# First batch, first stage: a transpose by VectorE out of PSUM in place of a trip through DRAM, with loads in one queue and weights rounded in pairs

## The chip, the cores and the metric

The kernel runs on one core of one Trainium2 chip. The metric is the time on the device in microseconds (us); lower is better. The executions of one kernel agree within about 0.2% on one chip.

## The reference, cut to what matters

```python
X = np.fft.rfft(x, axis=1)                 # x: (8, 3008, 256) float32
Y = X * (filt_r + 1j * filt_i)[None]       # one filter per frequency and channel
y = np.fft.irfft(Y, n=3008, axis=1)
h = y.reshape(24064, 256) @ w_in           # w_in  (256, 2048), float64
out = (h / (1 + np.exp(-h))) @ w_out       # w_out (2048, 256), float64
```

The transform of 3008 = 47 x 64 points is done as matmuls with tables. Stage 1 transforms over the rows, `forward` and the filters work on six groups g = 0 to 5 of residues, `inverse`, `even` and `rows` go back, and stage 3 makes y. The two matmuls of the experts follow. They make up most of the program, and batches 1 to 7 of the transform are woven into them. Only batch 0 must be through its transform before the first expert matmul (px) can start. The weights come as 64-bit floats and are made 32-bit on the chip ("rounded") while batch 0 runs: 16 pieces, of which 0 to 8 are done before px.

## The kernel before: the parts that matter

Stage 1 of batch 0 wrote its result to DRAM (d1) and read it back, which is how the data changed from "row on partitions" to "n on partitions":

```python
def stage1(u):                             # u = 0..7, batch 0
    ... two matmuls into PSUM, ps[0], ps[1]
    for h in range(2):
        evac(t1[:, h], ps[h])              # VectorE or ScalarE
    for par in range(2):
        nc.gpsimd.dma_start(out=d1[par]..., in_=t1[64 * par:64 * par + 2 * NS]...)
def load_t2(g):
    for par in range(2):
        nc.sync.dma_start(out=t2s[g][64 * par:64 * par + 64], in_=d1[par, 4 * g:4 * g + 4]...)
```

The order of the start:

```python
part["load_first"]()                       # x
idle(6)                                    # dummy matmuls, for TensorE's clock: 0.75 with, 0.70 without (e7_idle)
nc.sync.dma_start(out=d_t[:, 0:8], ...)
load_filters((nc.sync, nc.sync), 0, 4)     # the filters of g = 0, 1: 16 loads
weights(0, 1, 2)                           # loads of raw weights
for u in range(8):
    part["stage1"](u)
...
for j in range(3):
    rounded(j)                             # beside the trip through DRAM
idle(16)
for g in range(NG):
    forward, multiply, add of g
    if g == 0:
        load_filters((nc.sync, nc.gpsimd), 4, 2 * NG)   # 16 loads, half of them by GpSimd
        ...; load_t2(2), load_t2(3); weights(3, 4, 5)
    ...
    if g > 0:
        inverse_rows(part, g - 1)          # inverse, even, rows of the group before
    idle(2)
    if 1 <= g <= 4:
        rounded(g + 2)
```

`rows` stores the result of a group:

```python
queue = nc.gpsimd if b > 0 or (g == NG - 1 and i == 0) else nc.scalar
queue.dma_start(out=d2[a0:a0 + 4]..., in_=qt[:, a])
```

## Time and profile before

| | before |
|---|---|
| time, median of 3 | 2646.08 us (2644.95 to 2646.61) |
| span of the profiled run | 2644.6 us |
| PE (TensorE matmul) busy | 2587.3 us, 98% |
| DVE (VectorE) / ACT (ScalarE) / POOL (GpSimd) busy | 64% / 42% / 17% |
| first multiply by a filter (VectorE, g = 0) | 44.48 us |
| first expert matmul px | 127.53 us |
| from px to the end | 2517.1 us |

TensorE is full from px on, so a gain must come from what lies ahead of px. The last sixteen matmuls of stage 1, after a wait of 3.10 us for x, start 0.63 to 0.86 us apart from 17.03 to 20.95, and 0.43 apart from there on (granted clock 0.55 from 17.0 to 20.3 and 0.96 from 20.3 to 26.0); the prediction calls the slower ones cold. The profile's views of that stretch are shown in the prediction. In a timeline line the columns are start, duration, engine, line of the kernel, operation, output<-inputs and count; a bracket says how long the engine was idle before it and what ended that.

### The profile page before, as it was taken

What the parts mean: (1) busy time and instruction counts of PE and PEld (TensorE: products, weight loads), DVE (VectorE), ACT (ScalarE), POOL (GpSimd) and SP (SyncE); (2) the same over time, 40 slices, a digit from 0 to 9 for tenths busy, and PEclk for the clock granted to TensorE, in tenths of its full rate; (3) what the DMA queues carried; (4) which work ended last, traced back from release to release, by engine and by line L of the source; (5) the groups of instructions that cost most, each with busy time, mean ns of one, the idle gap of its engine ahead of it and who ended that gap; (6) DMA issues with size and microseconds to landing.
All of it is one profiled execution on the core that took longest, in us unless ns stands there. A gap on an engine that the chain in (4) does not pass through costs nothing.

```text
span 2644.6 us, 48073 instructions
## 1 busy us (share of the span) xinstructions
PE 2587.3 (98%) x18748; PEld 2189.9 (83%) x18748; DVE 1696.9 (64%) x3576; ACT 1110.4 (42%) x3026; POOL 450.4 (17%) x694
## 2 busy tenths in 40 slices
PE   6699999999999999999999999999999999999998
PEld 3378888888888888888888888888888888888987
DVE  3676766667666666666666676666766666555554
ACT  2354444443444444444444444444444444444443
POOL 4311111311121112112111211131112111100100
PEclk8699999999999999999999999999999999999999
DMA  8542222222223123321232222222223311211000
GB/s 247 166 114 51 77 66 51 75 72 66 56 72 84 45 64 79 70 65 47 76 71 56 65 75 67 51 71 70 72 56 72 81 48 28 55 22 21 9 16 16
DMA packets 203595, 176.29 MB, mean 67 GB/s; under 512 B 122148, under 2 KB 176772, under 8 KB 202772
## 3 DMA queue, kind: packets, MB, share of 16 engines
q1 hardware_dynamic: 183080, 121.57, 19.4%
q0 software_dynamic: 17616, 48.52, 5.8%
q8 instruction: 147, 2.41, 0.4%
q10 hardware_dynamic: 2672, 3.13, 0.4%
q14 instruction: 80, 0.66, 0.1%
HBM read 98.15 MB, written 84.41 MB: 69 GB/s over the span
## 4 chain that ended last, share of the span: by engine, by line
PE 94%; DVE 2%; DMA 2%; ACT 1%; issue 1%; POOL 1%; SPq 0%; DVEq 0%; ACTq 0%; POOLq 0%
PE acc L665 43%; PE px L606 25%; PE pyz L606 19%; PE pd L495 3%; PE pc L451 2%; PE pb L418 2%; PE pf L385 1%; DMA d_t<-d_tbl 1%; PE pa L327 0%; DMA raw<-in_moe_w_out_dram 0%; PE pa L318 0%; DVE g L577 0%; DMA d<-q 0%; ACT e L761 0%; DVE w_t L577 0%
## 5 line engine op out<-in xcount | busy, mean ns | idle before, releaser
L665 PE MATMUL acc<-g,w_t 128*128 128x256 f32 (+1 forms) x5376 | 1512.6, 375 | 0.4 <-DVE g L577 0.4
L665 PEld LDWEIGHTS acc<-g,w_t 128*128 128x128 f32 x5376 | 1022.5, 190 | 114.5 <-DVE g L577 0.8
L577 DVE TENSOR_TENSOR g<-pyz,abc 128x256 f32<-128x256 f32 (+1 forms) x1152 | 479.5, 416 | 545.0 <-ACT abc L627 302.2
L577 DVE TENSOR_TENSOR g<-g 128x256 f32<-128x256 f32 (+3 forms) x1152 | 616.3, 535 | 196.6 <-ACT g L610 183.5
L606 PE MATMUL px<-ty,w_t 128*128 128x256 f32 (+1 forms) x2304 | 687.0, 380 | 0.5 <-ACT abc L627 0.5
L610 ACT ACTIVATE g<-g 128x256 f32<-128x256 f32 (+1 forms) x1152 | 472.9, 411 | 247.6 <-DVE g L577 247.6
L577 POOL TENSOR_TENSOR s<-s 128x256 f32<-128x256 f32 (+1 forms) x329 | 259.7, 807 | 1452.6 <-DVE s L683 1417.0
L606 PEld LDWEIGHTS px<-ty,w_t 128*128 128x128 f32 x2304 | 424.5, 190 | 82.4 <-issue 25.2
L606 PE MATMUL pyz<-y,w_t 128*128 128x256 f32 (+1 forms) x1536 | 453.9, 377 | 2.6 <-DVE g L577 2.6
L606 PEld LDWEIGHTS pyz<-y,w_t 128*128 128x128 f32 x1536 | 283.7, 189 | 48.2 <-DVE g L577 8.1
L621 ACT COPY abc<-px 128x256 f32<-128x256 f32 (+1 forms) x384 | 141.3, 368 | 364.9 <-PE px L606 364.9
L610 ACT ACTIVATE g<-px 128x256 f32<-128x256 f32 (+1 forms) x384 | 145.8, 380 | 307.5 <-PE px L606 307.5
L627 ACT COPY abc<-px 128x256 f32<-128x256 f32 (+1 forms) x384 | 143.8, 374 | 309.9 <-PE px L606 309.9
L606 PE MATMUL px<-y,w_t 128*128 128x256 f32 (+1 forms) x768 | 229.9, 381 | 1.0 <-ACT y L246 1.0
L606 PE MATMUL pyz<-ty,w_t 128*128 128x256 f32 (+1 forms) x768 | 225.8, 376 | 0.0
L606 PEld LDWEIGHTS px<-y,w_t 128*128 128x128 f32 x768 | 142.2, 190 | 39.9 <-ACT g L610 15.5
L606 PEld LDWEIGHTS pyz<-ty,w_t 128*128 128x128 f32 x768 | 146.1, 190 | 16.8 <-DVE g L577 0.5
L614 ACT COPY abc<-px 128x256 f32<-128x256 f32 (+1 forms) x384 | 134.9, 351 | 2.7 <-PE px L606 1.3
L244 DVE COPY y<-pd 128x376 f32<-128x376 f32 x64 | 51.6, 806 | 103.8 <-PE pd L495 103.6
L246 ACT COPY y<-pd 128x376 f32<-128x376 f32 x64 | 51.7, 809 | 94.7 <-PE pd L495 94.7
L495 PEld LDWEIGHTS pd<-wi_t,t 48*64 48x64 f32 x4096 | 68.5, 139 | 26.2 <-issue 24.2
L495 PE MATMUL pd<-wi_t,t 48*64 48x47 f32 x4096 | 76.6, 237 | 5.9 <-issue 3.5
(76 smaller groups left out, 1362.5 us busy)
## 6 DMA issues: line engine op xcount, KB each, us to landing
t<-d SPq DMA_DIRECT2D x96, 256.0 KB
t<-d SPq DMA_DIRECT2D x128, 192.0 KB
d<-q POOLq DMA_DIRECT2D x85, 256.0 KB, 2.6
out_dram<-o SPq DMA_DIRECT2D x636, 32.0 KB
d<-tf POOLq DMA_DIRECT2D x144, 96.0 KB, 2.4
d<-t POOLq DMA_DIRECT2D x52, 192.0 KB, 3.4
xr<-in_x_dram SPq DMA_DIRECT2D x6, 1472.0 KB
x_all<-in_x_dram SPq DMA_DIRECT2D x72, 96.0 KB
```

Source lines behind the costliest of these rows:

```text
L244: nc.vector.tensor_copy(out=dst, in_=src)
L246: nc.scalar.copy(out=dst, in_=src)
L418: nc.tensor.matmul(out=ps[k][32 * j:32 * j + 32, ri, :], lhsT=d_t[rows, 4 * g + at, ri, :], rhs=t2[rows, at, :], start=True, stop=True)
L451: nc.tensor.matmul(out=ps[j][64 * k:64 * k + 64, a, :], lhsT=e_t[rows, g + a, k, ri, :], rhs=zs[k][rows, ri, :], start=(a == 0 and ri == 0 ...
L495: nc.tensor.matmul(out=ps[h][c0:c0 + 64, cb, i, :], lhsT=t4s[g][rows, i, 128 * cb + c0:128 * cb + c0 + 64], rhs=wi_t[rows, :], start=True, ...
L577: eng.tensor_tensor(out=out, in0=in0, in1=in1, op=op)
L606: nc.tensor.matmul(out=out, lhsT=w_t[:, c, 0, jp], rhs=rhs, start=start, stop=True, skip_group_check=True)
L610: nc.scalar.activation(out=g[:, k, 0:n], in_=g[:, k, 0:n] if src is None else src, func=AFT.Silu)
L614: nc.scalar.copy(out=sums[:, 0, 0:n], in_=xo)
L621: nc.scalar.copy(out=sums[:, 1, 0:n], in_=xo)
L627: nc.scalar.copy(out=sums[:, 2, 0:n], in_=xo)
L665: nc.tensor.matmul(out=acc[pair][i][:, h, 0:n], lhsT=w_t[:, c, 1, jp], rhs=g[:, k, 0:n], start=(jp == 0 and h == 0), stop=last, skip_group ...
```

## The change

The intent is to take the trip through DRAM out of batch 0's stage 1. A matmul now handles 16 channels for all 32 values of n, and VectorE transposes the 32x32 squares of the result straight from PSUM to SBUF. The result of stage 1 stays in the part of the weights' buffer w_t that is filled later, and so the layout of w_t changes. All early loads but two tables (ScalarE's) now stand in one queue (SyncE's) in order of need, the weights are rounded in pairs to overlap ScalarE's steps with VectorE's, VectorE places all rounded weights (GpSimd placed 0 to 6 before), and the dummy matmuls go. The core of the diff, cut:

```diff
-    w_t = cpool.tile([128, 7, 2, NJP, 128], FP32)
+    w_t = cpool.tile([128, NJP, 7, 2, 128], FP32)
...
+        def stage1_first(k):
+            ps = bank(b, f"pa_{b}_{k}")...rearrange("p (n c) -> p n c", c=16)
+            c0 = 16 * (k % 8)
+            for i in (0,) if k < 8 else (1, 2):
+                n0, n = ((0, 32), (0, 16), (16, 16))[i]
+                nc.tensor.matmul(out=ps[:, n0:n0 + n], lhsT=wx_t, rhs=xs[i][0:96, :, c0:c0 + 16], ...)
+            nc.vector.transpose(out=us["t2"][:, :, 16 * k:16 * k + 16].rearrange("p s c -> p c s"),
+                                in_=ps.rearrange("p n c -> p c n"))
...
-    def round_weights(j):
+    def round_weights(*js):          # the steps of two weights interleaved
...
-        eng = gp if j < 7 else v
-            eng.tensor_tensor(out=dst, ...)
+            v.tensor_tensor(out=dst, ...)
...
-    idle(6)
     load_filters((nc.sync, nc.sync), 0, 4)
-    weights(0, 1, 2)
-    for u in range(8):
-        part["stage1"](u)
-    for g in range(2):
-        part["load_t2"](g)
     nc.sync.dma_start(out=e_t, in_=e_dram.ap())
-    for j in range(3):
-        rounded(j)
-    idle(16)
+    nc.sync.dma_start(out=d_t[:, 8:NS], in_=d_dram[:, 8:NS])
+    load_filters((nc.sync, nc.sync), 4, 2 * NG)
+    weights(0, 1)
+    nc.sync.dma_start(out=wi_t, in_=wi_dram.ap())
+    weights(*range(2, 9))
+    for k in range(16):
+        part["stage1_first"](k)
     for g in range(NG):
...
-        idle(2)
-        if 1 <= g <= 4:
-            rounded(g + 2)
+        if g > 2:
+            rounded(2 * g - 6, 2 * g - 5)
...
-    rounded(7)
+    rounded(6, 7)
     rounded(8)
```

## The prediction

> **What bounds the kernel now.** I read the page first, then windows of 20 us over the start, then the chain of waits and the timeline there.
>
> The page's slices and its chain of work that ended last:
>
> ```profile
> PE   6699999999999999999999999999999999999998
> DVE  3676766667666666666666676666766666555554
> ...
> PE 94%; DVE 2%; DMA 2%; ACT 1%; issue 1%; POOL 1%; SPq 0%; DVEq 0%; ACTq 0%; POOLq 0%
> ```
>
> From the third slice (132 us on, a slice is 66 us) TensorE is full; that part of the program, some 2,510 us, is the expert matmuls with the later batches woven in. The diff touches there only the layout of w_t (each stationary is still one run of 128), and four stores in place of two of batch 1's stage 1. What can move is the start, where nothing is full:
>
> ```profile
> 0.00:20.00 20.00, 15.68 (x32) 8.37 (x33) 3.79 (x7) 3.83 (x6) 6.46 (x16) 0.93 0.91 248
> 20.00:40.00 20.00, 15.09 (x77) 9.21 (x75) 7.04 (x11) 7.82 (x12) 5.71 (x10) 0.93 0.91 274
> 40.00:60.00 20.00, 8.14 (x80) 4.20 (x74) 10.06 (x17) 3.44 (x6) 16.25 (x24) 0.67 0.75 206
> 60.00:80.00 20.00, 13.43 (x136) 5.75 (x134) 8.71 (x16) 6.31 (x12) 7.15 (x10) 0.59 0.98 282
> 80.00:100.00 20.00, 12.93 (x138) 5.57 (x136) 14.41 (x27) 6.77 (x13) 12.06 (x18) 0.69 0.15 54
> 100.00:120.00 20.00, 15.58 (x231) 11.67 (x234) 14.60 (x31) 7.56 (x12) 2.96 (x5) 0.74 0.62 142
> 140.00:160.00 20.00, 19.38 (x78) 14.16 (x77) 15.63 (x36) 11.51 (x29) 2.05 (x4) 1.00 0.35 106
> ```
>
> Columns: window, length, busy time of PE, PEld, DVE, ACT, POOL, granted PE clock, DMA share, GB/s. The DMA engines carry the first 80 us, VectorE the next 40; PE's busy time there includes the dummy "idle" matmuls. The chain in order of time names what the start waited for:
>
> ```profile
> 3.03 15.56 DMA d_t<-d_tbl
> ...
> 25.65 6.21 DMA raw<-in_moe_w_out_dram
> ...
> 60.65 4.99 DMA raw<-in_moe_w_out_dram
> 65.77 0.44 DVE m L757
> ...
> 121.56 3.45 issue
> ...
> 127.53 1.19 PE px L606 x2
> ```
>
> The first expert matmul (px) starts at 127.5 us. I take this as the end of the start: each us off it comes off the run. The timeline gives the largest hole of VectorE, from the end of its work on g = 0 and 1 at 53.4 to 65.8:
>
> ```profile
> 56.34 3.62 SPq L407 DMA_DIRECT2D t<-d  x4
> 65.77 0.43 DVE L757 TENSOR_SCALAR m<-raw 128x512 uint32<-128x512 uint32 x1 [12.41 <-DMA raw<-in_moe_w_out_dram]
> ```
>
> The loads of t2 for g = 2, 3 and, behind them in the same queue, the next raw weights are issued only at 56 to 63 us, after the filters, so VectorE stands still for 12.4 us.
>
> [...]
>
> ```profile
> L244 DVE COPY y<-pd 128x376 f32<-128x376 f32 x64 | 51.6, 806 | 103.8 <-PE pd L495 103.6
> L695 DVE STREAM_TRANSPOSE o<-s 128x256 f32<-128x256 f32 x192 | 73.7, 422 | 1.4 <-issue 1.0 <-DMA out_dram<-o 0.4
> ```
>
> Contiguous copies from PSUM take 425 ns for 256 elements and 691 for 512: 1.04 ns an element and 160 fixed, so 550 for 376. The y copy, whose writes step 128 bytes, takes 806: 1.72 ns an element. A transpose of 256 elements with whole lines takes 422, as a copy. [...]
>
> **The change part by part.**
>
> *Stage 1.* Removed: 16 evictions, 16 stores of t1 (3.1 MB), 12 loads of t2 (3.1 MB). Before, t2 arrives at 36.9 to 38.2, and VectorE, busy with weights 0 to 2, starts g = 0 at 44.5. Added: 16 transposes PSUM to SBUF, 512 elements each, reading at a step of 64 bytes and writing at 1 KB. By the y copy: 160 + 512 x 1.72 = 1.04 us; I take 1.1, as the strided PSUM read is new. Before, 1.5 MB of x had landed at 10.2 us and 3.1 MB at 17.0. Now half the channels (1.5 MB in 512-byte runs) must be in first: about 11 us. The first two matmuls are cold (2 x 0.85 each), the rest 0.86, below the transpose. First transpose at 13, sixteen end at 13 + 17.6 = 30.6; forward 0 takes 1.1 to 2; VectorE starts g = 0 at about 32, 12.5 earlier.
>
> *Loads.* All that g = 0 to 5 need is now ahead in one queue. The trace issues one in about 0.62 us, and waits once eight are in flight (the sixth filter went out when the third x landed, the seventh when the fourth did). So: filters of g 0, 1 issued by 25, e_t and d_t by 26.5, the other 16 filters by 36.5, raw 0 and 1 by 39.5, and landed some 2 later. g = 2 needs its filters at about 39.6: they just make it, so the 12.4 us hole closes.
>
> *VectorE from 32 us.* A group costs 4 multiplies at 0.60 and 4 row sums at 0.41, 4.1 in all (80.34 to 84.30 in the timeline). g = 0, 1 with the wait for POOL's adds and the inverse: 7.6, so 39.6; then 43.7 and 47.8 for g = 2, 3.
>
> *Roundings.* Before, one took 3.9 to 4.8 us of VectorE's order in the g loop, most of it waiting for ScalarE's four steps, and POOL placed the result. Now for a pair: ScalarE has six steps, 0.5 + 0.74 + 0.53 + 0.75 + 0.75 + 0.74 + 0.53 = 4.5 until the second mantissa; then 0.6 + 0.4 + 0.65 + 0.65 = 2.3 of VectorE; then four placings of 0.38, moved from POOL: 1.5. Sum 8.4, and up to 1 more [...] (0.95 against 0.42 in the old rounding 4). So pairing gains about 1.3 a pair and the moved placings give it back. But weights 0 to 2, rounded before under the DRAM trip, now lie in the path: some 13 us. Walk: pair (0,1) 56.3; g = 4 60.4; (2,3) 69.9; g = 5 with two adds 75.3; (4,5) 84.3; last row sums 86.0; (6,7) with its combine 97; (8) 101.5.
>
> *Tail.* From 86 the last d2 store waits on POOL for the combine to 87.2; before, 7.1 us went from that store's issue to the first stage-3 matmul, so 94.3, inside the roundings. The y copies wait for VectorE at 101.5 and px starts about 3.5 later, at 105. The 3.45 us "issue" gap may or may not come back.
>
> Sum: 12.5 (earlier start) + 12.4 (hole) + about 3.8 (two waits of 1.9 for POOL) + about 6 (slack by the y copies) + 2 (shorter waits), less 13 for the roundings put into the path and about 1 for the placings net of pairing: 22.5 us. 2646.1 - 22.5 = 2623.6.
>
> **Rivals.** (a) *The transposes are slower than a strided copy*: PSUM read and SBUF write penalties could add. At 1.7 us each stage 1 ends near 40, and 10 of the 22 are lost: about 2634. The even fit of the y copy on one strided side speaks for the lower cost; nothing in this trace strides a PSUM read. (b) *Loads bound instead*: without the DRAM trip VectorE may meet filters or raw weights that have not landed; one issue at 0.62 for 64 KB is only about 105 GB/s. Then g = 2 or pair (0,1) waits and the gain is 12 to 18: 2630. (c) *Roundings overlap better*: nothing of DVE's order changes, but if the contention with POOL goes, each pair is near 7.5 and stage 1 ends by 27: px near 92, 2610. (d) *Hidden anyway*: were the start off the path, 2646; the chain runs through it without slack, against this. (e) *Colder TensorE* without the dummies: pb and pc cost up to 1 us more per group, mostly beside VectorE.
>
> **Range and chances.** The terms' errors (stage 1 +-5, roundings +-5, loads -6, tail +-4) give 2612 to 2637 around 2624. 2% is 53 us; the start would have to shrink to 74 us, less than my VectorE sum alone, so faster has 0.03. A loss of 53 us would need a fault in the steady part: 0.02.
>
> **What would show it.** Right: transposes of about 1.0 to 1.2 us, no t store or t2 load before px, first multiply near 32, no VectorE hole over 5 us between it and px, a rounding pair of 8 to 9.5, px near 105, the time from px to the end unchanged within 5 us. Wrong: transposes near 1.7 or 0.7; VectorE waiting for filt or raw; a slower steady part, from the layout of w_t or batch 1's stores.

## The result, and the profile after

| | before | after |
|---|---|---|
| time, median of 4 | 2645.61 us (2644.95 to 2646.61) | 2632.71 us (2631.44 to 2633.54) |
| ratio | | 0.9950, 95% interval 0.9933 to 0.9968 |
| span of the profiled run | 2644.6 us | 2631.8 us |
| PE busy | 2587.3 us | 2554.9 us |
| first multiply by a filter | 44.48 us | 31.25 us |
| first expert matmul px | 127.53 us | 113.71 us |
| px to the end | 2517.1 us | 2518.1 us |

A ratio here and below is the mean time of one kernel's fast runs over that of the kernel before in the same rounds, so it is not quite the ratio of the medians quoted. The kernel is 12.9 us faster by the medians, half a per cent. The whole gain is ahead of px (13.8 us earlier), and the steady part is the same within 1 us. The predicted 2624 was too fast by 8.7 us; the range held.

The page after, its slices of 66 us and the engines of the chain that ended last:

```profile
PE   5599999999999999999999999999999999999998
DVE  5776766667666666666666666666766666555554
...
PE 94%; DVE 2%; DMA 1%; SPq 1%; ACT 1%; issue 1%; POOL 0%; DVEq 0%; ACTq 0%; POOLq 0%
```

TensorE has less to do in the first two slices (the dummies are gone), and the rest is as before. "SPq", the queue of SyncE, now has 1% of the chain where it rounded to 0% before, a first hint of what went otherwise than predicted. The same windows of the start (window, length, busy time of PE, PEld, DVE, ACT, POOL, PE clock, DMA share, GB/s):

```profile
20.00:40.00 20.00, 16.70 (x189) 10.98 (x195) 16.55 (x24) 0.65 (x2) 5.52 (x8) 0.85 0.58 174
40.00:60.00 20.00, 9.35 (x146) 3.52 (x130) 10.13 (x21) 4.67 (x10) 5.57 (x8) 0.72 0.89 296
80.00:100.00 20.00, 4.01 (x34) 1.76 (x34) 16.19 (x35) 8.05 (x14) 5.36 (x7) 0.50 0.28 83
100.00:120.00 20.00, 14.20 (x266) 11.09 (x267) 12.15 (x25) 7.14 (x12) 0.00 (x0) 0.51 0.91 228
140.00:160.00 20.00, 18.75 (x78) 14.14 (x77) 15.74 (x39) 9.51 (x24) 3.94 (x8) 1.00 0.33 93
```

VectorE is now busy in the windows 20 to 40 and 80 to 100 (16.55 and 16.19 of 20 us), but 40 to 60 has only 10.13: there is still a hole. VectorE's timeline shows stage 1 and the hole:

```profile
14.85 1.04 DVE L297 STREAM_TRANSPOSE w_t<-pa 128x512 f32<-128x512 f32 x1 [13.98 <-PE pa L295]
...
17.78 12.24 DVE L297 STREAM_TRANSPOSE w_t<-pa 128x512 f32<-128x512 f32 x14 [0.18 <-PE pa L295]
31.25 0.69 DVE L442 TENSOR_TENSOR z<-pb,filt 128x512 f32<-128x512 f32 x1 [1.24 <-PE pb L430]
...
47.28 0.69 DVE L442 TENSOR_TENSOR z<-pb,filt 128x512 f32<-128x512 f32 x1 [8.37 <-DMA filt<-in_filt_r_dram]
```

Stage 1 ends at 30.02, near the predicted 30.6. The multiply at 47.28 is the first of g = 2, and it stood 8.37 us for its filters. (Each of the 16 late loads fills 16 of the 128 partitions for g = 2 to 5, so g = 2 needs all of them.) The chain of waits says why they were late:

```profile
26.93 4.89 DMA d_t<-d_tbl
...
38.15 2.03 DMA d<-q
...
51.45 4.48 DMA raw<-in_moe_w_in_dram
...
93.71 2.54 DMA d<-q
98.58 6.02 DMA t<-d
104.73 1.09 PE pd L507 x29
105.82 4.09 issue
...
113.71 1.20 PE px L618 x2
```

The transfer "d<-q" at 38.15 is ScalarE's store of the rows of g = 0. It has nothing to do with the filters by its data, yet the chain goes through it to a load. It goes on by the raw weights of pair (0,1), which stand behind the filters in the same queue: they landed at 55.93, just as VectorE came to them (55.91), so they would have been the next wait. SyncE's queue at that point, from its timeline and, last, from its list of waits (us in total, times, longest):

```profile
34.63 0.60 SPq L233 DMA_DIRECT2D filt<-in_filt_i_dram  x1
40.20 0.58 SPq L233 DMA_DIRECT2D filt<-in_filt_r_dram  x1
```

```profile
SPq L233 <- DMA d<-q: 4.9, 1, 4.9
```

After its eighth late filter load SyncE stood still for 4.9 us until that store had landed, and then issued the other eight, one in about 0.62 us. The waits in the built program (its list of instructions) explain the link. The transfers of SyncE and ScalarE share eight completion semaphores, given out in turn in the order of the built program, and a new transfer waits until the last one on its semaphore is done. That order is not the source's: the build has ScalarE's first store between the second and the third late filter load. The ninth late filter load has semaphore 1, whose previous user is that store. The packed trace of this run agrees: the records of the two queues carry eight semaphore numbers between them, those of GpSimd's eight others, and the ninth late load waits for the number of the store at 38.15, which landed at 40.18; the load went out at 40.20.

At the end of the chain, "issue" of 4.09 us (105.82) is TensorE standing between two matmuls of stage 3 with nothing to wait for that the profile shows; before it was 3.45 us.

The groups that answer to those of before (busy us, mean ns):

```profile
L297 DVE STREAM_TRANSPOSE w_t<-pa 128x512 f32<-128x512 f32 x16 | 14.3, 1007 | 14.8 <-PE pa L295 14.8
L244 DVE COPY y<-pd 128x376 f32<-128x376 f32 x64 | 51.4, 805 | 102.2 <-PE pd L507 102.2
```

A transpose that follows a wait takes 1.04 us, as the timeline's first line has it. The 14 in a row are recorded with about 1.00 each, but they overlap at their ends: 14 in 12.24 us means that one starts every 0.86 us.

### The profile page after: what moved, and what is told of

It is laid out like the page before. It is cut to its first block, busy times and chain, and to the rows that moved or that the text cites.

```text
span 2631.8 us, 47869 instructions
## 1 busy us (share of the span) xinstructions
PE 2554.9 (97%) x18672; PEld 2170.0 (82%) x18672; DVE 1709.7 (65%) x3602; ACT 1098.9 (42%) x3008; POOL 435.1 (17%) x672
## 3 DMA queue, kind: packets, MB, share of 16 engines
q10 hardware_dynamic: 2928, 3.44, 0.4%
q8 instruction: 147, 2.41, 0.4%
## 4 chain that ended last, share of the span: by engine, by line
PE 94%; DVE 2%; DMA 1%; SPq 1%; ACT 1%; issue 1%; POOL 0%; DVEq 0%; ACTq 0%; POOLq 0%
PE acc L677 43%; PE px L618 25%; PE pyz L618 19%; PE pd L507 3%; PE pb L430 2%; PE pc L463 2%; PE pf L400 1%; DMA x_all<-in_x_dram 1%; PE pa L337 0%; SPq L233 0%; PE pa L328 0%; DVE g L589 0%; DVE w_t L804 0%; SPq L284 0%; DVE w_t L589 0%
```

## The experiments

There were twelve runs. "The changed kernel" has the ratio 0.9950 from its first measurement and 0.9945 as a control. Differences between kernels below are read from ratios and from the profiles, as the kernels ran on several chips.

### Where the hole on VectorE comes from

**e1_store_pool: the stores of g = 0 and 1 by GpSimd.**

```diff
-    queue = nc.gpsimd if b > 0 or (g == NG - 1 and i == 0) else nc.scalar
+    queue = nc.gpsimd if b > 0 or g < 2 or (g == NG - 1 and i == 0) else nc.scalar
```

> Edit: the stores of the inverse's rows for g = 0 and 1 go to GpSimd's queue in place of ScalarE's; nothing else. Theory (shared completion semaphores): the 8.4 us hole of VectorE before g = 2 comes from SyncE's ninth late filter load, which waits at 35.2 to 40.2 us for ScalarE's store of g = 0, because the loads of SyncE and the stores of ScalarE take turns on the same eight semaphores. Without ScalarE's stores in that sequence the late filters are all issued by about 40.5 and landed by 42.5: the hole shrinks to about 3.5 us, the first expert matmul comes at about 109 instead of 113.7, the time is about 2627.7. Rival (the loads are simply too slow: 0.62 us an issue, or bandwidth): the hole stays at 8 us and the time at 2632.7.

Measured: 2626.42 us (2625.73 to 2626.67), ratio 0.9921 (0.9908 to 0.9935). VectorE's wait ahead of g = 2, the ninth late filter load in SyncE's queue, and TensorE's gap in stage 3:

```profile
43.27 0.69 DVE L442 TENSOR_TENSOR z<-pb,filt 128x512 f32<-128x512 f32 x1 [4.50 <-DMA filt<-in_filt_r_dram]
33.58 0.59 SPq L233 DMA_DIRECT2D filt<-in_filt_r_dram  x1
```

```profile
103.37 2.90 PE L507 MATMUL pd<-wi_t,t 48*64 48x47 f32 x97 [2.17 <-issue]
```

One condition in one line takes 3.9 us off the hole (8.37 to 4.50), and px comes at 107.17. The ninth load goes out at 33.58 where it stood until 40.20. The loads and their order are untouched, so the wait was for the store and not for the data: the theory holds. Of the 6.5 us gained at px another 1.9 are TensorE's gap, which fell from 4.09 to 2.17.

**e2_filt_pool: the late filters by GpSimd, ahead of the groups.**

```diff
-    load_filters((nc.sync, nc.sync), 4, 2 * NG)
...
     for k in range(16):
         part["stage1_first"](k)
+        if k == 0:
+            gp.tensor_copy(out=warm, in_=w_t[:, 3, 3, 0, 0:1])   # waits for the first transpose
+            load_filters((nc.gpsimd, nc.gpsimd), 4, 2 * NG)
```

> Edit: the 16 late filter loads are issued by GpSimd, after a tiny copy that waits for the first transpose (16 us). Theory: they land by about 30, g = 2 waits for nothing, the whole hole of 8.4 us goes; first expert matmul near 105.5, time near 2624.5. Rival 1: these 2.1 MB compete with the rest of x and stage 1 ends late (after 32 instead of 30.1), which takes back 2 to 5 us. Rival 2: the hole only moves, to the raw weights 0 and 1 (they then must be there at 47.5): VectorE waits for raw instead, and the time stays above 2629.

Measured: 2630.55 us (2630.18 to 2631.45), ratio 0.9938 (0.9926 to 0.9951). This missed its expectation by 6 us. The hole moved:

```profile
49.18 1.66 DVE L482 TENSOR_TENSOR q<-q,pc 128x256 f32<-128x256 f32 x4 [4.51 <-ACT q L474]
```

In the built program SyncE's raw loads now come before the stores and have the semaphores that ScalarE's stores need. ScalarE's first two stores went out only from 46.76 to 48.74, when raw loads had landed, and its later copies, which VectorE needs, stood behind them: between two of ScalarE's copies 8.1 us passed. The first filters were late too (2.39 us at 35.16), with 16 more transfers beside them. So the shared semaphores strike in both directions, and a store held up on ScalarE holds ScalarE's computing as well.

**e8_act_half: e1, and half of the late filters by ScalarE at its start.**

```diff
-    load_filters((nc.sync, nc.sync), 4, 2 * NG)
+    load_filters((nc.sync, nc.scalar), 4, 2 * NG)
```

> The run with the first two groups' row stores on GpSimd's queue, and besides half of the late filter loads issued by ScalarE at its start in place of SyncE. Theory: what is left of VectorE's hole before g = 2 (4.5 us in the run with the stores moved alone) is nothing but 16 issues of 0.6 us in one queue; with 8 of them elsewhere the hole falls to 0 to 1 us, and the raw weights come 5 us earlier as well: first expert matmul near 103.5, time 2622 to 2624. Rival: a later stage holds it (the raw loads, the roundings, the last stores), the hole closes and the time stays at 2625 to 2627; or ScalarE's own copies are held up behind its loads, and it is slower than that.

Measured: 2629.27 us (2626.68 to 2631.10), ratio 0.9933 (0.9920 to 0.9947), behind e1. The hole ahead of g = 2 is 3.62 us, and px comes at 110.55 against 107.17 in e1. Stage 1 itself began later. Its first matmul came at 12.54 in e1, and here:

```profile
14.15 9.98 PE L295 MATMUL pa<-w_t,wx_t 96*128 96x512 f32 x18 [14.15 <-DMA w_t<-in_x_dram]
```

The first part of x landed 1.6 us later, with three filter loads that ScalarE issued from 1.80 to 3.17 us beside it, and the first multiply came at 32.92 in place of 31.12 in e1. That the three loads delayed x is argued from these times; no run separates it. Another 1.9 us of the 3.4 at px are TensorE's gap (4.09 here, 2.17 in e1). Both rivals that I had named were not quite it: half of the loads moved to the front took time from what was needed first.

**e9_split_pool: e1, and half of the late filters by GpSimd after the seventh transpose.**

```diff
+            if queues[j // 2] is None: continue          # in load_filters
...
-    load_filters((nc.sync, nc.sync), 4, 2 * NG)
+    load_filters((nc.sync, None), 4, 2 * NG)
...
         part["stage1_first"](k)
+        if k == 6:
+            gp.tensor_copy(out=warm, in_=w_t[:, 3, 3, 0, 0:1])
+            load_filters((None, nc.gpsimd), 4, 2 * NG)
```

> The run with the stores of the first two groups on GpSimd's queue, and besides half of the late filter loads issued by GpSimd after the seventh transpose of stage 1 (no load or store of this stretch is then left on ScalarE, and GpSimd's transfers have semaphores of their own, as the built program shows). Theory: the 4.5 us that remained of VectorE's hole before g = 2 are 16 issues of 0.6 us in one queue; with 8 of them elsewhere SyncE is done 5 us sooner, the hole falls under 1 us and px comes at 102.5 to 104 in place of 107.2: 2622 to 2624, ratio about 0.991. Rival: as with half of them on ScalarE, the extra loads delay the first filters or the raw weights, g = 2 or the first pair waits for those, and the ratio stays at 0.992.

Measured: 2625.61 us (2624.92 to 2627.00), ratio 0.9919 (0.9905 to 0.9932), px at 107.28. The hole is gone:

```profile
40.80 0.69 DVE L444 TENSOR_TENSOR z<-pb,filt 128x512 f32<-128x512 f32 x1 [0.79 <-DMA raw<-in_moe_w_in_dram]
```

The step expected of the hole came (0.79 us left), and g = 2 starts at 40.80, near the 39.6 of the prediction. Of the 3.7 us by which the hole is shorter, though, 1.2 are there because the groups came later; SyncE's last filter load is out 3.9 us earlier than in e1, and g = 2 starts 2.5 us earlier. And the time is e1's: the first multiply was 1.5 us later than in e1 (32.60 against 31.12), and TensorE's gap is 3.89 us again against 2.17. The control below, on the same chip, also starts 0.9 us later than the changed kernel's first profile, so more than half of that may be the chip or the run.

### The control

**c_after: the changed kernel again.**

> The changed kernel itself, unaltered, as a control in the same rounds as the combinations: 0.995 of the kernel before, as at first (0.9933 to 0.9968), and a profile with the same hole of 8.4 us on VectorE before g = 2 and a gap of about 4 us among TensorE's pd matmuls. If the gap differs from 4.1 us here, its size varies from run to run of one kernel and its differences between the experiments mean little.

Measured: 2632.55 us (2631.72 to 2634.55), ratio 0.9945 (0.9931 to 0.9958), hole 8.36 us, gap 3.82 us, px at 114.12, first multiply at 32.14. So between two profiles of one kernel the gap differs by 0.3 us and the start by 0.9.

### TensorE's gap in stage 3

**e3_early_loads: what is loaded beside stage 3, loaded before it.**

```diff
+    for u in range(2):                      # ahead of the loop over g
+        second["load_x"](u)
+    ... the loads of wf_t, wq_t
...
+        if g > 3:
+            weights(2 * g + 1, 2 * g + 2)   # 9 to 12, within the loop
...
-    for u in range(2):                      # after the loads of t4
-        second["load_x"](u)
-    ...
-    weights(9, 10, 11, 12, 13)
+    weights(13)
```

> Edit: batch 1's first two x loads and the tables wf, wq are issued right after the raw weights 0 to 8, and raw weights 9 to 12 inside the loop over g, so that little is loaded while stage 3 runs. Theory [...]: the 4.1 us gap of TensorE in stage 3 that no engine explains (105.8 to 109.9) goes, and the last t4 load lands sooner; first expert matmul at about 109, time about 2628. Rival [...]: it stays at 3.5 to 4 us with quiet DMA engines, and the time at 2632 +-1. The hole before g = 2 must stay as it is (8 us) under both.

Measured: 2631.64 us (2631.09 to 2632.72), ratio 0.9942 (0.9930 to 0.9955), px at 112.40, hole 8.36:

```profile
108.61 2.90 PE L507 MATMUL pd<-wi_t,t 48*64 48x47 f32 x97 [2.25 <-issue]
```

The gap is neither gone nor as it was. I had expected it gone or 3.5 to 4 us, and it is 2.25. This run alone does not show that the data queues set its length: e1 and e5, whose loads beside stage 3 are those of the changed kernel, have gaps as short (2.17 and 2.52).

The gap is always there, so I looked for what it has in common in all fourteen profiles. In each one packet of an instruction queue ("q8 instruction: 1, 0.02" in the view of DMA traffic, which does not say for which engine) moves near it; the page has 147 such packets with 2.41 MB, 16 KB each. Read to a quarter of a microsecond (last column: from the packet's quarter to the end of the gap):

| kernel | gap starts | length | packet | gap ends after packet |
|---|---|---|---|---|
| before | 121.56 | 3.45 | 122.50 | 2.5 |
| after | 105.82 | 4.09 | 106.75 | 3.2 |
| c_after | 106.51 | 3.82 | 107.50 | 2.8 |
| e1_store_pool | 101.20 | 2.17 | 100.50 | 2.9 |
| e2_filt_pool | 104.41 | 4.09 | 105.75 | 2.8 |
| e3_early_loads | 106.36 | 2.25 | 105.50 | 3.1 |
| e4_strides | 104.95 | 4.36 | 106.25 | 3.1 |
| e5_singles | 108.88 | 2.52 | 108.25 | 3.2 |
| e6_place_pool | 107.38 | 3.62 | 108.00 | 3.0 |
| e7_idle | 106.08 | 3.44 | 106.75 | 2.8 |
| e8_act_half | 102.66 | 4.09 | 103.75 | 3.0 |
| e9_split_pool | 99.59 | 3.89 | 100.75 | 2.7 |
| e10_split_idle | 99.92 | 3.78 | 100.75 | 3.0 |
| e11_all | 99.42 | 1.02 | 97.50 | 2.9 |

The gap ends 2.5 to 3.2 us after the packet in every one. It is long (3.4 to 4.4 us) where the packet came after TensorE had run dry and short (1.0 to 2.5) where it came before. Its place is also fixed in the stream of instructions, not in time. Before it stand 591 matmul records and 591 weight loads in each of the ten profiles without dummies, 716 and 716 in the kernel before, and 718 and 718 in the three with dummies. The difference of 125 to 127 pairs is 250 to 254 instructions. Set against the 147 packets of that queue, the 37,344 records of matmuls and weight loads on the page after (37,496 on the page before) are 254 to 255 a packet: if all these packets carry TensorE's instructions, which is my estimate, the places of the gap lie one packet apart. The gap costs 1.0 to 4.4 us on the path. That it is the wait for such a packet fits all of this, but no view says which engine the packets are for and no run moved the packet alone, so it is a likely cause and not one that was shown.

**e7_idle: the dummy matmuls back.**

```diff
+    idle(20)                                # ahead of stage 1
     for k in range(16):
         part["stage1_first"](k)
...
+        idle(2)                             # in each of the six groups
...
     inverse_rows(part, NG - 1)
+    idle(12)
```

> The changed kernel with dummy matmuls put back: 20 before stage 1, 2 a group, 12 ahead of stage 3 (44 in all). Theory: they keep TensorE's clock up; the first stage-1 matmuls take 0.43 in place of 0.85 us, which VectorE's transposes at 1.04 hide but for the first (0.4 to 0.9 us), and the pb and pc groups are up to 0.5 us shorter each, of which VectorE hides most: 0.5 to 2 us faster, about 2631.5. Rival: the dummies are only in the way (20 at the start can be later than x): 0 to 2 us slower. Besides: if TensorE's 4 us gap among the pd matmuls sits at a fixed number of instructions, it comes some 44 matmuls earlier than after the 97 pd matmuls of that group's label (159 pd records before it), near 115.

Measured: 2633.32 us (2631.00 to 2635.72), ratio 0.9948 (0.9936 to 0.9961), the same as the changed kernel. In the profile the first multiply comes 2.0 us earlier (29.22) and px at 112.33, 1.4 us earlier, since most of the gain is eaten by a longer hole:

```profile
45.95 0.69 DVE L442 TENSOR_TENSOR z<-pb,filt 128x512 f32<-128x512 f32 x1 [9.71 <-DMA filt<-in_filt_r_dram]
```

The mean granted clock from the start to the end of the gap is 0.75 (718 matmul records, the dummies counted), where the changed kernel has 0.70 (591). The 1.4 us are not seen in the median. My side expectation on the gap was wrong: it did not come earlier in stage 3 but 39 pd records later, which is 127 records later in the whole stream with the dummies counted, by the estimate above one packet further.

### The roundings

**e5_singles: each weight rounded alone.**

```diff
-            rounded(2 * g - 6, 2 * g - 5)
+            rounded(2 * g - 6)
+            rounded(2 * g - 5)
...
-    rounded(6, 7)
+    rounded(6)
+    rounded(7)
```

> The changed kernel, but each weight tile is rounded alone, as before, instead of in pairs (placings stay on VectorE, loads untouched). Theory of the prediction: pairing lets ScalarE's steps of one tile run beside VectorE's steps of the other and saves about 1.3 us a pair, on the path in at least the four pairs after g = 3, 4, 5 and at the end. Then this kernel takes 4 to 6 us longer than the changed one, about 2637 (a single of 4.3 us as (8) shows, twice that is 8.6 against pairs of 8.0 to 8.6, would say less). Rival: the pairs measured at 8.0 to 8.6 us are no shorter than two singles at 4.3, so the pairing is worth nothing and this run comes out within 1 us of the changed kernel, 2632 to 2634.

Measured: 2634.48 us (2633.26 to 2636.22), ratio 0.9954 (0.9941 to 0.9966), px at 115.19. Between the two expectations. In the profile the stretches from the first step of two weights to the next work are, in pairs, 8.20, 8.56, 8.00 and 9.81 us (the last with a combine), and singly 8.94, 9.84, 8.74 and 10.54. Pairing gains 0.7 to 1.3, together 3.5 us. At px it is 1.5, because the gap was 2.52 in place of 4.09 (115.19 - 2.52 against 113.71 - 4.09 is 3.1 us). What the single form waits for in each weight is ScalarE:

```profile
58.39 0.69 DVE L790 SCALAR_TENSOR_TENSOR scratch<-raw,scratch 128x512 f32<-128x512 uint32 x1 [1.03 <-ACT scratch L783]
```

**e6_place_pool: the placings of weights 0 to 5 back on GpSimd.**

```diff
-            v.tensor_tensor(out=dst, ...)
+            eng = gp if j < 6 else v
+            eng.tensor_tensor(out=dst, ...)
```

> The changed kernel with the placings of weights 0 to 5 back on GpSimd, as in the kernel before. Theory: each pair costs VectorE 1.5 us less (four placings of 0.38), three pairs, so up to 4.6 us less on VectorE's path; GpSimd takes 1.4 us a tile for it [...]. If VectorE's order is what the start waits for, the first expert matmul comes 2 to 4 us earlier: 2629 to 2631. Rival: GpSimd's combines of weights and adds of rows come later by what it takes, the roundings wait for it [...], and the time is within 1 us of the changed kernel or above it.

Measured: 2632.59 us (2629.91 to 2634.11), ratio 0.9945 (0.9933 to 0.9958), the control's. The rival holds for the time, but VectorE is not where it was lost. From g = 2 to the end of (8) VectorE takes 56.9 us (48.48 to 105.35) where the changed kernel takes 58.6, though some steps are slower beside GpSimd: of the first four of pairs (2,3), (4,5) and (6,7), which take 0.42 us alone, eleven take 0.75 to 0.95, where the changed kernel has five such. (In the kernel before, the two opening steps of a rounding take 0.43 and 0.42 us from 65.77, with GpSimd idle, and 0.93 and 0.95 from 75.57, beside its adds.) What takes the gain back is the last store of rows, which GpSimd issues. The chain:

```profile
89.26 2.97 POOL w_t L805 x4
...
95.90 2.48 DMA d<-q
```

GpSimd places pair (4,5) from 89.26, sums the weights after it, and only then issues the store, at 95.90 in place of 93.71; stage 3 waits for that store, and TensorE runs dry at 107.38 in place of 105.82. So moving the placings to VectorE cost nothing in time and gained nothing.

### The price of the transpose

**e4_strides (relative error 0.40).** The sixteen transposes take four forms of operands, four times each, to part the cost of the strided read from that of the strided write. Its output is wrong, which doesn't matter for the time.

```diff
+            if k // 4 % 2:   # contiguous write
+                dst = us["t2"]...[:, 512 * k:512 * k + 512].rearrange("p (c s) -> p c s", s=32)
+            if k // 8:       # contiguous read
+                src = ps...rearrange("p (c n) -> p c n", n=32)
+            nc.vector.transpose(out=dst, in_=src)
```

> Wrong result on purpose: the sixteen transposes are four of each kind: 0 to 3 as in the change (PSUM read at a step of 64 bytes, SBUF written at a step of 1 KB), 4 to 7 with contiguous writes, 8 to 11 with contiguous reads, 12 to 15 with both contiguous. If only the strided write costs (as the y copy suggested): 1.04, 0.69, 1.04, 0.69 us. If only the PSUM read costs: 1.04, 1.04, 0.69, 0.69. If each does alone and they overlap: 1.04, 1.04, 1.04, 0.69. If a transpose of this form costs 1.04 by itself: 1.04 four times.

Measured: 1.04 us with both strided, 0.72 with only the write made contiguous, 1.00 with only the read made contiguous, 0.72 with both. The last:

```profile
28.59 0.72 DVE L304 STREAM_TRANSPOSE w_t<-pa 128x512 f32<-128x512 f32 x1
```

So the penalty lies wholly on the SBUF side, 0.3 us for 512 elements that each go to another row of 1 KB. The read of PSUM at a step of 64 bytes costs nothing that shows: the 1.00 against 1.04 is the place in the row, as in the changed kernel those in a row take 1.00 with both strided.

### Combinations

**e10_split_idle: e9 with the dummies of e7.**

> The kernel of the run before (stores and half of the late filters on GpSimd) with the 44 dummy matmuls put back. With the hole at g = 2 gone the 2.0 us that the dummies gained at the first multiply are no longer eaten by it: 1 to 2 us faster than without them, 2621 to 2623. Rival: the filters of g = 2 bound again, since the groups come earlier, and the dummies give nothing.

Measured: 2625.40 us (2625.16 to 2625.58), ratio 0.9917 (0.9904 to 0.9931): no measurable difference from e9. The first multiply comes 2.9 us earlier (29.71 against 32.60), g = 2 only 0.7 (40.10 against 40.80), with 2.81 us of idle time ahead of it. The profile puts that idle time down to a dummy matmul here and to a raw load in the next run, where it is 2.67; the filters of g = 2 are my guess, and it stays open.

**e11_all: e10 with the early loads of e3.**

> The kernel of the run before (stores and half of the late filters on GpSimd, dummies back) and besides the x loads of batch 1, two tables and weights 9 to 12 loaded before stage 3, as in the run with early loads. In all ten profiles read so far TensorE's gap in stage 3 ends 2.3 to 3 us after the one packet of 16 KB in the instruction queue has moved, and it is 2.2 to 2.5 us long where that packet moved before the gap began, 3.4 to 4.1 where it moved about 1 us after. Theory: with the data queue emptier the packet moves early and the gap falls from 3.8 to about 2.2; px at 104.5 to 105.5, 2623.5 to 2624.5, ratio 0.9910 to 0.9915. Rival: the early loads delay the last stores and t loads, and px stays at 106.5 or later.

Measured: 2622.25 us (2621.16 to 2623.39), ratio 0.9910 (0.9893 to 0.9926), px at 103.26. It is better than expected:

```profile
100.44 1.94 PE L509 MATMUL pd<-wi_t,t 48*64 48x47 f32 x58 [1.02 <-issue]
```

The instruction packet moved at 97.5, 1.9 us before TensorE ran dry, and the gap is down to 1.02. Of the 3.3 us that px gained on e10, 2.8 are the gap. This kernel is faster than both: about 24 us than the kernel before and, by the two medians, 10 us than the changed one (the ratios 0.9910 and 0.9945 on two chips say 9).

## Why the prediction was right or wrong

The prediction walked VectorE from stage 1 to px, so it can be checked at each stop (us from the start; the walk gave starts and ends, the profile after is read at the same points):

| stop | predicted | after | off by |
|---|---|---|---|
| stage 1 ends | 30.6 | 30.02 | -0.6 |
| first multiply, g = 0 | 32 | 31.25 | -0.8 |
| first multiply, g = 2 | 39.6 | 47.28 | +7.7 |
| pair (0,1) done | 56.3 | 64.11 | +7.8 |
| pair (2,3) done | 69.9 | 76.63 | +6.7 |
| pair (4,5) done | 84.3 | 90.32 | +6.0 |
| last row sums done | 86.0 | 91.89 | +5.9 |
| pair (6,7) done | 97 | 101.70 | +4.7 |
| (8) done | 101.5 | 105.90 | +4.4 |
| px | 105 | 113.71 | +8.7 |

**Stage 1 came out right, in part by luck.** A transpose that follows a wait takes 1.04 us, which is the figure drawn from the y copies before the 1.1 that was used, but in a row they start 0.86 us apart. The first one, put at 13, came at 14.85, as x was in at 12.7 and not at 11. From the first to the end it took 15.2 us and not 17.6, so the two errors nearly cancel, and g = 0 starts 13.2 us earlier where 12.5 were predicted. Run e4 adds that the extrapolation was right for the reason given, the strided write (1.04 us, and 0.72 with a contiguous one), and that the fear of the strided read, rival (a), had no ground (1.00 with a contiguous one, which those in a row take with both strided).

**The loads step failed.** It read "g = 2 needs its filters at about 39.6: they just make it, so the 12.4 us hole closes". The schedule was right up to the loads of e_t and d_t (issued at 26.30 and 26.93, predicted "by 26.5"). From there the step counted only SyncE's own transfers against the eight in flight. The built program shows that ScalarE's stores and loads take their turn on the same eight semaphores. So a load of filters was tied to a store that cannot run before g = 0 is through VectorE. The hole went from 12.41 us to 8.37 rather than to nothing. Run e1 shows 3.9 us of that to be the wait for the store. The other 4.5 are for the larger part the length of one queue, 0.6 us an issue and short waits between: with eight of the loads on GpSimd's queue (e9) g = 2 starts 2.5 us earlier and 0.8 of hole is left, but 1.2 us of the difference are there because the groups came later, and with earlier groups 2.7 to 2.8 stand there again (e10, e11). The 16 late filters were predicted issued by 36.5; even with the store out of the way (e1) the last went out at 39.3. Rival (b), loads bound instead, with 12 to 18 us of gain, is what happened; its cause as put, the issue rate, is half of it.

The tie could be read from the kernel before. The prediction read its hole as loads that were issued "only at 56 to 63 us, after the filters". But SyncE was done with its half of the filters and d_t at 48.1, and its list of waits has what came next (us in total, times, longest):

```profile
SPq L407 <- DMA d<-q: 9.2, 2, 8.2
```

The loads of t2 for g = 2 stood 8.2 us for ScalarE's store of g = 0, whose semaphore they share in that build too. Had the raw weights behind them gone out these 8.2 us earlier, some 4 of the 12.4 us would have been left (an estimate; no run did it). The change removed those loads of t2 and left the wait to other loads.

**The roundings were right.** Pairs of 8.0 to 8.6 us lie at the low end of the predicted 8 to 9.5, which with shorter groups gave back 3.3 us between g = 2 and (8). Their parts were less good: pairing gains 0.7 to 1.3 us a pair (e5), not 1.3 each, and the moved placings, put at 1.5 us a pair, cost VectorE 1.7 us in all and nothing at px (e6), because with them on GpSimd the last store goes out 2.2 us later.

**The tail failed by its gap.** The last store went out at 93.71, where the prediction had 87.2, and t4 arrived at 104.73, still inside the roundings. From the end of (8) to px it took 7.8 us and not 3.5. The step "The 3.45 us 'issue' gap may or may not come back" left it out of the sum and counted 6 us of slack by the y copies as gain. It came back with 4.09, after 591 matmul records in place of 716. In e11, where the gap is 1.02, the stretch is short again.

**The rest.** The steady part did not move (rival: none), rival (c) did not happen, and rival (e) costs VectorE at most 2.0 us at the first multiply and nothing in the time (e7). Put together (the terms of the prediction's sum add up to 22.7, its walk to px gives 22.5): 22.5 predicted, less 8.4 for the hole and 4.1 for the gap, plus some 4 for stops that were faster than walked, is about 14, and px came 13.8 earlier.

## What to carry to other kernels

Where loads and stores of two engines share completion semaphores, the order of the program ties a load to an unrelated store (here SyncE's queue stood 4.9 us for one): before relying on an early load, list which transfer had its semaphore before, and put a store that must wait for computing on a queue with semaphores of its own (GpSimd's here, which took 3.9 us off the hole in e1). Where a queue stands still in the trace before the change, ask what it waits for, as the change may carry that wait along (8.2 us before, 4.9 after). A single queue of small loads has a rate (here 0.6 us an issue), so "all loads early in one queue" is a plan only after the issues are counted up to the moment of need, with the waits between them. A gap that the profile calls issue, at one place of the instruction stream, is a term to carry in the sum, since it need not go away when the work ahead of it gets shorter (here 3.45 us before and 4.09 after).
